# Other start addresses in SBUF for the softplus buffers, the staging buffers and the attention tiles

## The chip, the core and the metric

The kernel runs on one core of one Trainium2 chip. The metric is the device time of one execution in microseconds (us); a kernel's time is the median of several runs. The profile of one further execution shows where the time goes.

## The reference

Attention in chunks of 64 tokens (8 batches, 8 heads, 576 tokens, head size 64), and on its output, 4608 tokens by 512, a feed-forward layer with a softplus between two matrix products:

```python
scores = scale * np.matmul(q_c, k_c.transpose(0, 1, 2, 4, 3))   # chunks of 64 by 64
scores = scores - np.max(scores, axis=-1, keepdims=True)
attn = np.exp(scores)
attn = attn / (np.sum(attn, axis=-1, keepdims=True) + 1e-09)
out = np.matmul(attn, v_c)
...
h = x @ w_in                                                    # 4608x512 by 512x2048
g = np.maximum(h, 0.0) + np.log1p(np.exp(-np.abs(h)))           # softplus
return (g @ w_out).astype(np.float32)                           # 4608x2048 by 2048x512
```

## The kernel before

The tokens are cut into 9 macro tiles of 512, the 2048 columns of the hidden layer into 16 slices of 128. A block is one macro tile with one slice; there are 144. In each block TensorE makes two groups of matmuls. `gemm1` (line 567) makes a 128x512 piece of h: 12 matmuls, whose stationary operands (weights) are 128x128 pieces of w_in, in the tiles `wi_hi`, `wi_lo` or `wib`, and whose moving operands are pieces of `x`, the attention's output. `gemm2` (line 600) multiplies that block's softplus with w_out: 12 matmuls, whose weights are 128x128 pieces of `g_hi` and `g_lo`, and whose moving operands are rows of w_out (`wo_hi`, `wo_lo`, `late`, `wo_end`), 128x512. Each value stands as a sum of two float32r numbers, a high part and a low part, hence three matmuls for each product. (The first block is cut in two halves, `a0` and block 0.)

Between the two, ScalarE makes `u`, the softplus (line 578), and rounds it to `g_hi` (line 582), and VectorE or GpSimd takes the difference `g_lo` (line 586). `g_hi` and `g_lo` have two buffers each, `u` has one. TensorE's order is fixed: gemm1 of block n+1, then gemm2 of block n.

Attention works on tiles of 128 tokens by 512 (8 heads of 64). The first four are made at the start, in tiles that later hold weights (`late`, `x`). The others go through the loaded tiles `q` and `k`, the transposed ones `qe` and `ka` and the transposed probabilities `eT`. Their 64x64 matmuls stand between gemm1 and gemm2 of some blocks, as a burst (lines 449 and 530): the scores of two tiles and the output of the two before. A burst takes both buffers of the PSUM tile `pa`, which gemm1 takes as well. VectorE frees them with a maximum (line 494), a rest of x (line 546) and a subtraction (line 499).

Weights come in 32 loads into three staging buffers `raw` (lines 234 and 239), are put together in `top` and `low` (or `wib`) and rounded into their places (lines 247 to 286). The output is staged in `raw` too.

A planner with a table of costs makes the order of the instructions of all engines when the kernel is built; the addresses of tiles play no part in it. Pools of tiles lie one behind the other in each partition of SBUF, in the order in which they are opened, each tile rounded up to 32 bytes:

```python
later = ctx.enter_context(tc.tile_pool(name="later", bufs=2))
late = ctx.enter_context(tc.tile_pool(name="late", bufs=LATE))
const = ctx.enter_context(tc.tile_pool(name="const", bufs=1))
xpool = ctx.enter_context(tc.tile_pool(name="xpool", bufs=4))
ld = ctx.enter_context(tc.tile_pool(name="ld", bufs=1))
att = ctx.enter_context(tc.tile_pool(name="att", bufs=1))
sp = ctx.enter_context(tc.tile_pool(name="sp", bufs=2))
```

Of the kernel before, what the change touches and what calls it, by code (L numbers as in the profile page):

```python
# [11 lines left out]
F32 = mybir.dt.float32  # L12
F32R = mybir.dt.float32r
I32 = mybir.dt.int32
# [3 lines left out]
BF16 = mybir.dt.bfloat16  # L18
# [129 lines left out]
def chunked_attention_softplus_ffn(  # L148
# [12 lines left out]
    P = 128  # L161
# [14 lines left out]
    UW = 512  # L176
    RAW_BUFS = 3
# [2 lines left out]
    FILL = 0.8  # L180
    LATE = 15
    STAGED = 15

    later = ctx.enter_context(tc.tile_pool(name="later", bufs=2))
    late = ctx.enter_context(tc.tile_pool(name="late", bufs=LATE))
# [2 lines left out]
# [3 lines that stand above are left out]
# [5 lines left out]
    ident = const.tile([P, P], F32, name="ident")  # L196
    make_identity(nc, ident)
    half = DF // 2
    wi = [tuple(const.tile([P, KC, half], F32R, name=n) for n in ("wi_hi", "wi_lo"))]
    stage = [later.tile([P, KC * half], F32, name="wib") for _ in range(2)]  # L200
    wo_hi = const.tile([P, HALF_FC, DM], F32R, name="wo_hi")
# [19 lines left out]
    live = {}  # L221

    def raw_tile():
        return ld.tile([P, 2 * UW + 2], I32, name="raw", bufs=RAW_BUFS)

# [1 line left out]
    def w_load(u, is_in, fc):  # L229
        queue = nc.gpsimd if u in LOAD_POOL else nc.sync  # L230
        raw = raw_tile()
        st = raw.bitcast(U16)[:, 1 : 4 * UW + 1]
        if is_in:
            queue.dma_start(
                st.rearrange("p (c f) -> p c f", c=KC),
                w_in_v[:, :, 4 * fc * P : 4 * (fc + 1) * P],
            )
        else:
            queue.dma_start(st, w_out_v[:, fc, :])
        live["raw", u] = raw  # L240

    def w_top(u):
        live["top", u] = tops[0]
        tops.append(tops.pop(0))
        top = live["top", u].bitcast(F16).rearrange("p (f t) -> p f t", t=2)[:, :, 1]
        src = live["raw", u].bitcast(BF16)[:, 4:].rearrange("p (f t) -> p f t", t=4)[:, :, 0]
        (nc.gpsimd.tensor_copy if u not in TOP_ACT else nc.scalar.copy)(top, src)  # L247

    def w_low(u):
        if u < STAGED:  # L250
            o = u * UW
            low = stage[o // (KC * half)][:, o % (KC * half) :][:, :UW].bitcast(I32)
        else:
            low = ld.tile([P, UW], I32, name="low", bufs=LOW_BUFS)
        src = live.pop(("raw", u)).bitcast(U32)[:, 1 : 2 * UW + 1].rearrange("p (f t) -> p f t", t=2)[:, :, 0]
        nc.scalar.activation(low, src, AF.Copy, scale=2.0**-13)
        live["low", u] = low
# [347 lines left out]
    def evacuate(w, t):  # L605
        if t % 2 == 0:
            live["out", w["m"], t // 2] = raw_tile()
        o = live["out", w["m"], t // 2][:, t % 2 * DM : (t % 2 + 1) * DM].bitcast(F32)
        (nc.vector.tensor_copy if t % 2 else nc.scalar.copy)(o, pos[w["m"]][t])
        live["o", w["m"], t] = o  # L610
# [55 lines left out]
    for u, (g, is_in, fc) in enumerate(units):  # L666
        (of_in if is_in else of_out)[fc] = u
        d = due(g) - 4
        last = [f"w_hi{u}", f"w_lo{u}"]
        users = []  # L670
        if not is_in and fc >= HALF_FC:
            for j in range(2 * (fc - HALF_FC), min(2 * (fc - HALF_FC) + 2, LATE)):
                users.append("EVVSS"[j % 5] + str(j // 5))
        pl = "POOL" if u in LO_POOL else "DVE"
        ph_ = "POOL" if u in HI_POOL else "ACT"
        staged = u < STAGED
        pool = u in LOAD_POOL
        plan.add(f"load{u}", "POOL" if pool else "SP", 0.75 if pool else 0.55, partial(w_load, u, is_in, fc),
                 urg=d - LEAD if u else LQ, kb=480,
                 take=[("raw", [f"w_top{u}", f"w_low{u}"])], after=[LOAD_AFTER])  # L680
        on_act = u in TOP_ACT
        plan.add(f"w_top{u}", "ACT" if on_act else "POOL", 0.78 if on_act else 0.77, partial(w_top, u), [f"load{u}"],
                 urg=d, take=[("top", [f"w_add{u}"])])
        plan.add(f"w_low{u}", "ACT", 0.67, partial(w_low, u), [f"load{u}"], urg=d + 0.01,
                 take=[] if staged else [("low", last)], after=[f"w_top{u}"])
        plan.add(f"w_add{u}", "DVE", 0.68, partial(w_add, u), [f"w_top{u}", f"w_low{u}"], urg=d + 1.4, port=True)
        freed = []
        if is_in and fc == HALF_FC:
            freed = [f"w_{n}{j}" for n in ("hi", "lo") for j in range(STAGED)]
        if fc:  # L690
            freed.append(f"w_hi{(of_in if is_in else of_out)[fc - 1]}")
        plan.add(last[0], ph_, 0.63 if ph_ == "POOL" else 0.61, partial(w_hi, u, is_in, fc),
                 [f"w_add{u}"] + users + freed, urg=d + 2.1)
        plan.add(last[1], pl, 1.3 if pl == "POOL" else 0.65, partial(w_lo, u, is_in, fc, pl == "POOL"),
                 [last[0]] + users, urg=d + 2.8)
# [111 lines left out]
    for w in ahead + blocks:  # L807
        g, m, fc, name = w["g"], w["m"], w["fc"], w["name"]
# [58 lines left out]
```

## Time and profile before

| | |
|---|---|
| Time, median of 3 runs | 878.07 us (876.37 to 879.29) |
| The profiled execution's own time | 878.49 us |
| Its span, from the first to the last instruction | 876.7 us |
| TensorE (PE) matmuls | busy 861.6 us, 98% of the span |
| VectorE (DVE), ScalarE (ACT), GpSimd (POOL) | busy 348.5, 309.4 and 65.3 us |
| DMA engines | 31.9% of the span |

PE's share of busy time says little by itself: matmuls overlap, and each is shown from its start to a modelled end. How fast TensorE goes is read from the distance between the starts of matmuls that follow each other.

### The profile page before, as it was taken

How to read it: one execution, taken by the hardware profiler on the slowest of the kernel's cores; microseconds unless marked ns; L12 is line 12 of the kernel's file. 1: busy time of each engine (PE TensorE's matmuls, PEld its weight loads, DVE VectorE, ACT ScalarE, POOL GpSimd, SP SyncE). 2: the span in 40 equal slices, each digit the busy share in tenths (PEclk: the TensorE clock that was granted, in tenths of full speed). 3: DMA queues.
4: the chain of work that ended last, by engine and by line, in shares of the span. 5: the costliest groups of instructions: out<-in, count | busy, mean ns of one | idle time of the engine just before them, and what ended most of it. 6: DMA issues, size and time to landing. Idle time of an engine off the chain costs nothing.

```text
span 876.7 us, 14820 instructions
## 1 busy us (share of the span) xinstructions
PE 861.6 (98%) x5874; PEld 701.5 (80%) x5874; DVE 348.5 (40%) x589; ACT 309.4 (35%) x483; POOL 65.3 (7%) x68
## 2 busy tenths in 40 slices
PE   8799999999999999999999999999999999999998
PEld 7677888888888888888888888888888888888886
DVE  5999964333424161525242342334241614121111
ACT  4576744332423242424242332324232424222222
POOL 0564741000000000000000000000000000000000
PEclk9999999999999999999999999999999999999999
DMA  9787753322232224231322223122322241000001
GB/s 223 186 210 218 174 146 90 67 40 49 42 96 43 49 42 104 35 63 29 71 70 56 43 47 97 39 50 42 96 42 51 41 105 33 17 29 20 1 1 48
DMA packets 209958, 63.65 MB, mean 73 GB/s; under 512 B 187105, under 2 KB 203233, under 8 KB 209889
## 3 DMA queue, kind: packets, MB, share of 16 engines
q1 hardware_dynamic: 209888, 62.71, 31.9%
q8 instruction: 46, 0.75, 0.4%
q14 instruction: 24, 0.19, 0.1%
HBM read 45.09 MB, written 9.44 MB: 62 GB/s over the span
## 4 chain that ended last, share of the span: by engine, by line
PE 89%; DMA 4%; DVE 4%; SPq 1%; issue 1%; ACT 1%; POOL 0%; DVEq 0%; POOLq 0%; ACTq 0%
PE po L600 42%; PE pa L567 41%; PE pa L530 2%; DMA raw<-in_moe_w_in_dram 2%; PE pa L449 2%; DMA raw<-in_moe_w_out_dram 1%; PE po L330 1%; DVE wib L261 1%; SPq L322 1%; DVE mx L494 0%; DVE den L510 0%; DMA q<-in_q_dram 0%; DMA x<-in_v_dram 0%; DVE g_lo L586 0%; DVE x L546 0%
## 5 line engine op out<-in xcount | busy, mean ns | idle before, releaser
L578 ACT ACTIVATE u<-pa 128x512 f32<-128x512 f32 (+1 forms) x145 | 86.2, 594 | 510.1 <-PE pa L567 505.4
L586 DVE TENSOR_TENSOR g_lo<-u,g_hi 128x512 fp32r<-128x512 f32 (+1 forms) x137 | 94.9, 693 | 295.3 <-ACT g_hi L582 295.0
L567 PE MATMUL pa<-x,wib 128*128 128x512 f32 x864 | 208.6, 390 | 0.0
L567 PEld LDWEIGHTS pa<-x,wib 128*128 128x128 f32 x864 | 161.7, 188 | 36.0 <-PE po L600 2.4
L567 PE MATMUL pa<-x,wi_hi 128*128 128x512 f32 (+1 forms) x584 | 179.3, 389 | 2.1 <-DVE x L546 2.1
L600 PE MATMUL po<-late,g_hi 128*128 128x512 f32 x540 | 172.1, 394 | 0.0
L567 PEld LDWEIGHTS pa<-x,wi_hi 128*128 128x128 f32 x584 | 109.9, 189 | 24.3 <-DVE x L546 2.3
L600 PEld LDWEIGHTS po<-late,g_hi 128*128 128x128 f32 x540 | 101.2, 187 | 24.4
L567 PE MATMUL pa<-x,wi_lo 128*128 128x512 f32 (+1 forms) x292 | 114.0, 390 | 1.3 <-POOL top L247 1.0
L600 PE MATMUL po<-wo_hi,g_lo 128*128 128x512 f32 x288 | 114.9, 399 | 0.0
L600 PE MATMUL po<-late,g_lo 128*128 128x512 f32 x288 | 114.6, 398 | 0.0
L600 PE MATMUL po<-wo_lo,g_hi 128*128 128x512 f32 x288 | 114.0, 396 | 0.0
L600 PE MATMUL po<-wo_hi,g_hi 128*128 128x512 f32 x288 | 113.5, 394 | 0.0
L582 ACT CAST g_hi<-u 128x512 fp32r<-128x512 f32 (+1 forms) x145 | 89.4, 616 | 4.4
L567 PEld LDWEIGHTS pa<-x,wi_lo 128*128 128x128 f32 x292 | 55.2, 189 | 15.7 <-PE po L600 2.9
L600 PEld LDWEIGHTS po<-wo_hi,g_lo 128*128 128x128 f32 x288 | 54.3, 188 | 13.1
L600 PEld LDWEIGHTS po<-wo_hi,g_hi 128*128 128x128 f32 x288 | 54.1, 188 | 13.2
L600 PEld LDWEIGHTS po<-late,g_lo 128*128 128x128 f32 x288 | 54.0, 187 | 13.0
L600 PEld LDWEIGHTS po<-wo_lo,g_hi 128*128 128x128 f32 x288 | 54.1, 188 | 12.8
L494 DVE TENSOR_REDUCE mx<-pa 128x8 f32<-128x512 f32 x32 | 22.0, 686 | 69.4 <-ACT x L542 69.0
L426 DVE STREAM_TRANSPOSE qe<-q 128x512 f32<-128x512 f32 x29 | 20.5, 707 | 65.5 <-DMA k<-in_k_dram 46.3
L426 DVE STREAM_TRANSPOSE ka<-k 128x512 f32<-128x512 f32 x29 | 20.6, 711 | 51.1 <-DMA k<-in_k_dram 33.8
(101 smaller groups left out, 565.9 us busy)
## 6 DMA issues: line engine op xcount, KB each, us to landing
out_dram<-raw SPq DMA_DIRECT2D x36, 256.0 KB, 2.4
raw<-in_moe_w_in_dram SPq DMA_DIRECT2D x16, 512.0 KB, 5.0
raw<-in_moe_w_out_dram SPq DMA_DIRECT2D x16, 512.0 KB, 5.0
eT<-ka SPq DMA_DIRECT2D x248, 32.0 KB, 1.9
q<-in_q_dram SPq DMA_DIRECT2D x232, 32.0 KB, 2.2
k<-in_k_dram SPq DMA_DIRECT2D x232, 32.0 KB, 2.1
q<-in_v_dram SPq DMA_DIRECT2D x60, 64.0 KB, 2.5
k<-in_v_dram SPq DMA_DIRECT2D x60, 64.0 KB, 2.5
```

Of the source, the lines that this page charges most:

```text
L261: nc.vector.tensor_tensor(low, low, live.pop(("top", u)), op=ALU.add)
L322: nc.sync.dma_start(dv[a * C : (a + 1) * C, :, c2, :], v[b, a * HP : (a + 1) * HP, c * C : (c + 1) * C, :].rearrange("h s d -> s h d"),)
L330: nc.tensor.matmul(dst[:, :P], ident, ident, start=True, stop=True)
L426: nc.vector.transpose(t, live.pop((n, i)))
L449: nc.tensor.matmul(pa[o, c2, col : col + C], qT[r, a * HP + hl, :], kT[r, a * HP + hl, :], start=True, stop=True,)
L494: nc.vector.tensor_reduce(mx, sc, axis=AX.X, op=ALU.max)
L530: nc.tensor.matmul(pa[o, a, col : col + C], vt[r, 4 * j + 2 * h2 + c2, :], eT[r, :, 4 * c2 + 2 * j + h2, :], start=True, stop=True,)
L567: nc.tensor.matmul(ph, wt[:, c, fs], x[:, ts_, c, :], start=(n == 0), stop=(n == 3 * KC - 1))
L578: nc.scalar.activation(w["u"], w["ph"], AF.Softplus)
L582: nc.scalar.copy(w["hi"], w["u"])
L586: (nc.gpsimd if pool else nc.vector).tensor_tensor(w["lo"], w["u"], w["hi"].bitcast(F32), op=ALU.subtract)
L600: nc.tensor.matmul(pos[w["m"]][t], gg[:, ts_], wt, start=(w["first"] and n == 0), stop=(w["last"] and n == 2),)
```

## The change

Three edits of address alone. Each `raw` buffer gets 14 columns (56 bytes) more, which nobody reads or writes; with that the bounds of one slice in `w_top` are written out. Ahead of the softplus buffers stands a tile of 192 bytes, `pad`, which nobody uses. No instruction is added, dropped or moved: the instructions of every engine, with their waits, stand in the same order as before.

```diff
     STAGED = 15
+    G_PAD = 48
...
     half = DF // 2
+    sp.tile([P, G_PAD], F32, name="pad", bufs=1)
...
     def raw_tile():
-        return ld.tile([P, 2 * UW + 2], I32, name="raw", bufs=RAW_BUFS)
+        return ld.tile([P, 2 * UW + 16], I32, name="raw", bufs=RAW_BUFS)
...
-        src = live["raw", u].bitcast(BF16)[:, 4:].rearrange("p (f t) -> p f t", t=4)[:, :, 0]
+        src = live["raw", u].bitcast(BF16)[:, 4 : 4 * UW + 4].rearrange("p (f t) -> p f t", t=4)[:, :, 0]
```

What it does to the addresses follows from the sizes. The first pool begins at byte 16512 of each partition, which is 32 times 512 and 128 over. All tiles up to the staging buffers are multiples of 512 bytes, so they all stand at remainder 128 by 512.

| Tiles | Remainder by 512 before | after | Remainder by 64 before | after |
|---|---|---|---|---|
| `wib`, `late`, `wi_hi`, `wi_lo`, `wo_hi`, `wo_lo`, `wo_end`, `top`, `x` | 128 | 128 | 0 | 0 |
| `raw`, three buffers (4104 bytes, then 4160) | 128, 160, 192 | 128, 192, 256 | 0, 32, 0 | 0, 0, 0 |
| `q`, `k`, `low`, `eT`, `qe`, `ka` (2048 bytes) | 224 | 320 | 32 | 0 |
| `u`, `g_hi`, `g_lo` (2048 bytes) | 352 | 128 | 32 | 0 |

## Rows read from the trace of the kernel before

**Rows 1.** The page's chain of work that ended last: shares of the span by engine.

```profile
PE 89%; DMA 4%; DVE 4%; SPq 1%; issue 1%; ACT 1%; POOL 0%; DVEq 0%; POOLq 0%; ACTq 0%
```

**Rows 2.** Timeline of PE from 137.5 us: start, length, line, tiles; both in us.

```profile
137.50 0.39 PE L600 MATMUL po<-wo_hi,g_lo 128*128 128x512 f32 x1
...
138.20 0.40 PE L600 MATMUL po<-wo_hi,g_lo 128*128 128x512 f32 x1
...
138.90 0.39 PE L600 MATMUL po<-wo_hi,g_lo 128*128 128x512 f32 x1
...
139.60 0.40 PE L600 MATMUL po<-wo_hi,g_lo 128*128 128x512 f32 x1
...
140.29 0.39 PE L567 MATMUL pa<-x,wi_lo 128*128 128x512 f32 x1
...
140.97 0.39 PE L567 MATMUL pa<-x,wi_lo 128*128 128x512 f32 x1
...
141.65 0.39 PE L567 MATMUL pa<-x,wi_lo 128*128 128x512 f32 x1
...
142.33 0.39 PE L567 MATMUL pa<-x,wi_lo 128*128 128x512 f32 x1
...
143.02 0.39 PE L600 MATMUL po<-wo_hi,g_lo 128*128 128x512 f32 x1
```

**Rows 3.** The chain that ended last, in order of time: start, length (us).

```profile
213.95 3.00 PE po L600 x12
216.94 2.98 PE pa L567 x12
219.93 2.79 PE po L600 x12
222.72 2.73 PE pa L567 x12
...
730.14 2.98 PE pa L567 x12
```

**Rows 4.** Windows, instructions of line 600 alone: stretch, its length, busy (count).

```profile
84.00:877.00 793.00, 406.28 (x1644) 306.92 (x1644) 1.00 0.27 59
```

**Rows 5.** Timeline of all engines around 80 us; in brackets idle time and its releaser.

```profile
81.62 1.28 PE L530 MATMUL pa<-eT,x 64*64 64x64 f32 x29 [0.59 <-DMA x<-in_v_dram]
...
84.20 0.51 PE L530 MATMUL pa<-eT,x 64*64 64x64 f32 x19 [0.59 <-DMA x<-in_v_dram]
```

**Rows 6.** Timeline of all engines from 400 us: a subtraction, and gemm1 behind it.

```profile
402.75 0.68 DVE L499 TENSOR_TENSOR qe<-pa,mx 128x512 f32<-128x512 f32 x1
...
403.57 2.99 PE L567 MATMUL pa<-x,wib 128*128 128x512 f32 x12
```

**Rows 7.** Timeline of all engines from 406 us: the softplus of a block.

```profile
406.65 0.60 ACT L578 ACTIVATE u<-pa 128x512 f32<-128x512 f32 x1 [5.43 <-PE pa L567]
...
407.94 0.69 DVE L586 TENSOR_TENSOR g_lo<-u,g_hi 128x512 fp32r<-128x512 f32 x1 [3.19 <-ACT g_hi L582]
...
411.93 0.39 PE L600 MATMUL po<-late,g_lo 128*128 128x512 f32 x1
```

**Rows 8.** Timeline of POOL at 107 us: low weights of slice 13.

```profile
107.32 1.30 POOL L286 TENSOR_TENSOR wib<-low,wib 128x512 fp32r<-128x512 f32 x1
```

**Rows 9.** Timeline of PE at 110 us: gemm1 of slice 13.

```profile
110.14 1.07 PE L567 MATMUL pa<-x,wib 128*128 128x512 f32 x4
```

**Rows 10.** Groups of instructions of VectorE: busy us, mean ns, then idle time.

```profile
L546 DVE TENSOR_TENSOR x<-pa,x 128x512 fp32r<-128x512 f32 x36 | 23.2, 680 | 0.0
...
L609 DVE COPY raw<-po 128x512 f32<-128x512 f32 x18 | 11.7, 680 | 3.1 <-PE po L600 3.1
```

**Rows 11.** Timeline of PE from 13 to 22 us: the 64x64 matmuls of the scores.

```profile
15.29 1.09 PE L364 MATMUL po<-late 64*64 64x64 f32 x30
...
20.61 1.09 PE L364 MATMUL po<-ka,qe 64*64 64x64 f32 x30
```

**Rows 12.** DMA issues up to 130 us: count, KB each, median us to landing.

```profile
q<-in_q_dram SPq DMA_DIRECT2D x32, 32.0 KB, 3.9
...
x<-in_q_dram SPq DMA_DIRECT2D x8, 32.0 KB, 3.8
```

## The prediction

> **What bounds the kernel now.** I read the chain of work that ended last first. The reader is to see that TensorE alone makes 89% of it [rows 1]: apart from the start, the time is the distance between matmuls, added up. So the next view is the timeline of TensorE in a quiet stretch, and there not the lengths, which are modelled, but the starts [rows 2]. They stand three matmuls apart. In gemm1 three steps take 0.68 us, 0.2267 us each: 140.29, 140.97, 141.65, 142.33. In gemm2 three steps take 0.70 us, 0.2333 us each: 137.50, 138.20, 138.90, 139.60. Both groups stream 512 columns with a weight load for each matmul, so they should go at one pace, and gemm2 doesn't.
>
> The last three steps of each group tell on what that hangs. Those of gemm2, up to the first matmul of gemm1, take 0.69 us (139.60 to 140.29), less than its others. Those of gemm1, up to the first matmul of gemm2, take 0.69 us too (142.33 to 143.02), more than its others. In the last step of a group the moving operand is still its own, and the weights being loaded meanwhile are those of the next group. So the longer step goes with weights that come from `g_hi` and `g_lo`, and not with the moving operand or with the PSUM bank written. One block (137.50 to 143.02) takes 5.52 us; at gemm1's pace throughout, 8 times 0.68, it would take 5.44. That is 0.08 us in each of the 144 blocks.
>
> What sets weights in g apart from those in `wi_hi`, `wi_lo` and `wib` is their address: remainder 352 by 512 bytes, which is 32 by 64, against 128, which is 0 by 64. Both are 128x128 float32r with 512 bytes in a row in each partition. They also lie at the upper end of SBUF and were written shortly before, which the change leaves as it is.
>
> **The change, part by part.** No instruction, wait or DMA is added or moved, so every term is a duration that may change with an address.
>
> *The softplus buffers, 352 to 128.* The step with weights from g at remainder 128 isn't in the trace. From below I bound it by gemm1's 0.2267 us, whose weights stand at 128, from above by today's 0.2333 (nothing gained). I take 0.2267, since the last steps of gemm2 come nearest to the new state, `wo` moving and weights at 128 being loaded, and they go at the faster pace within what 0.01 us resolves: 0.69 for two slow steps and a fast one. Gain: 0.08 us a block, where TensorE is what the block waits for.
>
> *Where it isn't.* At 81.62 and 84.20 us TensorE waits 0.59 us each for v from HBM [rows 5]; whatever the blocks ahead save, it would wait longer there. Behind 84 us stand 1644 of gemm2's 1728 matmuls [rows 4], or 137 blocks. Behind twelve bursts gemm1 takes 2.92 to 2.98 us instead of 2.73, the first at 216.94 and the last at 730.14 [rows 3]: it needs a `pa` buffer, and begins at 403.57, right behind the subtraction that reads that buffer until 402.75 + 0.68 = 403.43 [rows 6]. That subtraction stands in a VectorE chain which the end of the burst starts, so gemm2 in between may go faster and gemm1 begins no earlier. Those twelve blocks gain nothing. There remain 125 blocks by 0.08, 10.0 us.
>
> *Does something else become late?* The softplus of a block begins at 406.65, `g_lo` is there at 408.63, and its gemm2 begins at 411.93 [rows 7]: 3.3 us to spare, and a block shortens by 0.08. While weights come in, the tightest place I found is slice 13: its low part is ready at 108.62 [rows 8], and gemm1 needs it at 110.14 [rows 9], 1.5 us later. Seven blocks between 84 and 126 us bring TensorE 0.6 us forward, so the cover holds; if it were gone at once, these seven would gain nothing, 0.6 us of the sum.
>
> *Staging, q, k, probabilities.* VectorE writes 128x512 from PSUM in 680 ns into `x` (remainder 128) and in 680 ns into `raw` (128, 160 and 192 mixed) [rows 10]. Thirty 64x64 matmuls of the scores take 1.09 us out of `late` at 128 and 1.09 us out of `ka` and `qe` at 224 [rows 11]. Loads of q in small pieces land after 3.8 us in `x` and 3.9 us in `q` at 224 [rows 12], in stretches of different load. I take nothing for all of these. As bounds, 0.1 us on such a load is hidden where q and k are loaded many blocks ahead; ahead of 84 us, where TensorE does wait for DMA, ten such loads in a row would be 1 us either way.
>
> *Sum.* The profiled execution takes 878.49 us, 876.7 of span and 1.8 around it. Less 10.0 that is 868.5. It stands 0.4 us above the median of 878.07, so I predict a median of 868.1 us.
>
> **Rows against the skill.** The trace has weights loaded from g going with a step longer by 0.0067 us. The Trainium skill, "TensorE: Matmul & The Clock Gate", section "Step-by-step: what each phase is for", says that TensorE reads weights and moving operand through two independent ports, so that loading the next weights takes no bandwidth from the running matmul. By that rule an address of g would cost nothing and the sum would be 0; the trace's last steps of a group speak against it. The same skill, "SBUF — State Buffer", section "Specifications (TRN2)", gives lines of 16 bytes. Both 352 and 128 are multiples of 16, so by that too nothing would change; no row here separates 16 bytes from 64.
>
> **The rivals.**
>
> 1. *No change, about 878.1 us.* The slower step belongs to g for another reason than its remainder: its place at SBUF's end, or that it is written and read within one block. For it: the scores' 64x64 matmuls go equally fast at remainders 128 and 224 [rows 11], which differ by 32 bytes beyond a multiple of 64 just as 128 and 352 do. Against it: each of these uses a quarter of the array, four in turn, so a longer load may be hidden behind the other three, and they load half the columns only. The two rules of the skill above would end here. Chance 0.10.
>
> 2. *Half, about 873 us.* Two things add up in g's 0.0067 us, and the remainder is one of them: 125 blocks by 0.04 are 5.0 us. Nothing in the rows shows two parts. Chance 0.08.
>
> 3. *Slower, about 888 us.* Now both streams of gemm2 stand at the same remainder by 512. If weights and moving operand then collide, a step becomes longer than today's 0.2333 us. If it grew by as much again as it now lies above gemm1's, 125 blocks by 0.08 would come on top. It decides from any step over 0.2333 on. Against it: gemm1 has weights at 128 and `x` at 128 or 384 (pieces of 256 bytes) and takes the faster step throughout, and in the last step of gemm2 both are at 128. Chance 0.05.
>
> 4. *The gain is made and eaten by waits* that I hold for covered: only the seven blocks above, 868.7 us; it belongs to the forecast.
>
> **How the numbers follow.** The forecast has the rest, 0.77, and by the spread of runs (876.4 to 879.3, 1.7 below and 1.2 above the median) its own range is 866.4 to 869.7. If the early and the twelve blocks gain as well, 144 by 0.08 are 11.5 us, which with that spread ends at 865.0. Upwards I go to 874.0, which takes in the half case and 1 us of it for loads at the start. That leaves out no change and slower, 0.15, and a little below. A change of 0.3% (2.6 us) is what a measurement of this kernel can tell from none. Faster by more than that: 0.77 + 0.08 = 0.85. Within: 0.10. Slower: 0.05.
>
> **What would show it.** In the profile after, three steps of gemm2 take 0.68 us like those of gemm1, also across the border between the two; a pair of gemm1 and gemm2 in the chain takes 5.44 us, not 5.52. The twelve gemm1 behind bursts begin as late behind their burst as now, so these are longer, by up to 0.08 us. The groups of ScalarE and VectorE keep their means within 10 ns, and the waits for v stay, together longer by some 0.6 us, the saving of the seven blocks ahead of them. If gemm2's three steps still take 0.70 us, the remainder isn't the cause and the prediction fails; if they shrink and the time doesn't, a wait has taken the gain, and the list of gemm1's late starts must show where.

## The result and the profile after

The changed kernel takes 868.39 us (median of 4 runs, 866.78 to 870.07) beside 877.35 us before (4 runs): ratio 0.9895, 95% interval 0.9866 to 0.9925. The forecast was 868.1 us and faster. The profiled execution took 869.51 us, 867.7 of span, against 878.49 and 876.7.

The page's chain, shares by engine, answers to [rows 1]; TensorE is still what everything else is hidden behind:

```profile
PE 88%; DMA 5%; DVE 4%; ACT 1%; issue 1%; SPq 1%; POOL 0%; DVEq 0%; POOLq 0%; ACTq 0%
```

The timeline of PE in the same stretch as [rows 2] (start and length in us; gemm1 is now line 569, gemm2 line 602):

```profile
137.40 0.39 PE L602 MATMUL po<-wo_hi,g_lo 128*128 128x512 f32 x1
...
139.44 0.39 PE L602 MATMUL po<-wo_hi,g_lo 128*128 128x512 f32 x1
...
140.12 0.39 PE L569 MATMUL pa<-x,wi_lo 128*128 128x512 f32 x1
...
142.84 0.39 PE L602 MATMUL po<-wo_hi,g_lo 128*128 128x512 f32 x1
```

Nine steps of gemm2 take 2.04 us (137.40 to 139.44), where they took 2.10 (137.50 to 139.60 in [rows 2]). The three steps across the border to gemm1 take 0.68 (139.44 to 140.12). The twelve of gemm1, its border included, take 2.72 (140.12 to 142.84) instead of 2.73 (140.29 to 143.02). The chain in order of time answers to [rows 3]:

```profile
213.11 2.94 PE po L602 x12
216.10 2.99 PE pa L569 x12
219.09 2.72 PE po L602 x12
221.81 2.72 PE pa L569 x12
...
400.50 2.99 PE pa L569 x12
```

A block is 2.72 + 2.72 = 5.44 us instead of 5.52. The gemm1 behind a burst is as late as before. VectorE's two rests of x and its subtraction ahead of that gemm1 are these rows of its timeline:

```profile
398.47 1.28 DVE L548 TENSOR_TENSOR x<-pa,x 128x512 fp32r<-128x512 f32 x2
399.67 0.68 DVE L501 TENSOR_TENSOR qe<-pa,mx 128x512 f32<-128x512 f32 x1
```

The subtraction ends at 400.35, and gemm1 begins 0.15 us behind it, at 400.50; in [rows 6] it was 0.14 us.

### The profile page after: what moved, and what is told of

It reads as the page before. It is cut to its first block, busy times and chain, and to the rows that moved or that the text cites. A ratio compares the mean times of both kernels' runs of the same rounds, so it can differ in the third digit from the quotient of the medians.

```text
span 867.7 us, 14820 instructions
## 1 busy us (share of the span) xinstructions
PE 850.9 (98%) x5874; PEld 701.5 (81%) x5874; DVE 347.6 (40%) x589; ACT 309.9 (36%) x483; POOL 64.7 (7%) x68
## 4 chain that ended last, share of the span: by engine, by line
PE 88%; DMA 5%; DVE 4%; ACT 1%; issue 1%; SPq 1%; POOL 0%; DVEq 0%; POOLq 0%; ACTq 0%
PE pa L569 42%; PE po L602 42%; DMA raw<-in_moe_w_out_dram 3%; PE pa L532 2%; PE pa L451 1%; DMA raw<-in_moe_w_in_dram 1%; DMA eT<-ka 1%; DVE wib L263 1%; PE po L332 1%; DVE g_lo L588 0%; SPq L324 0%; ACT u L580 0%; DVE mx L496 0%; DVE low L263 0%; DMA k<-in_v_dram 0%
## 5 line engine op out<-in xcount | busy, mean ns | idle before, releaser
L602 PE MATMUL po<-late,g_hi 128*128 128x512 f32 x540 | 169.5, 390 | 0.0
```

The source lines that it names most:

```text
L602: nc.tensor.matmul(pos[w["m"]][t], gg[:, ts_], wt, start=(w["first"] and n == 0), stop=(w["last"] and n == 2),)
```

## The experiments

All are the changed kernel with the edit shown; the last has none. The theories A, B, P and R are named in the expectations. The distance named below is that from the moving operand's start to the weights' start, by 128 bytes: 96 before the change (352 less 128), 0 after. Experiments of one group ran beside the same runs of the kernel before.

**1. The pad alone** (`e1_pad_only`)

```diff
-    G_PAD = 48
+    G_PAD = 72
...
-        return ld.tile([P, 2 * UW + 16], I32, name="raw", bufs=RAW_BUFS)
+        return ld.tile([P, 2 * UW + 2], I32, name="raw", bufs=RAW_BUFS)
```

> Only the softplus buffers move, to remainder 128 by 512; raw, q, k, low, qe, ka and eT stay where they were before. If the whole gain comes from weights read out of g (my theory), three steps of gemm2 take 0.68 us and the time is that of the changed kernel, 868 us, within 2 us. If the staging buffers or q, k and the probabilities have a part in it, it lies above that by their part: over 870 us.

Measured: 870.39 us, just over the 870 us that the expectation set as the limit, beside 878.36 before. The ratio is 0.9895 (0.9876 to 0.9913), that of the whole change. Its timeline of PE, nine steps of gemm2 in 2.04 us:

```profile
138.83 0.39 PE L602 MATMUL po<-wo_hi,g_lo 128*128 128x512 f32 x1
...
140.87 0.39 PE L602 MATMUL po<-wo_hi,g_lo 128*128 128x512 f32 x1
```

From gemm2 of block 14 to the end the span is 741.4 us here (869.2 less 127.80) and 741.3 in the first profile after (867.7 less 126.39), so from there on the whole gain is made. The gain is that of g's place; the wider staging buffers and the new places of q, k and the probabilities have no part in it that these runs could show.

**2. The staging buffers alone** (`e2_raw_only`)

```diff
-    sp.tile([P, G_PAD], F32, name="pad", bufs=1)
```

> The wider raw buffers without the pad: everything but g as in the changed kernel, and u and g at remainder 448 by 512, which is 0 by 64 but not that of w_out's tiles. Theory A (what counts is a start at a multiple of 64 bytes): three steps of gemm2 take 0.68 us, 868 us. Theory B (what counts is the same remainder by 512 as the other operand): 0.70 us, 877 to 878 us.

Measured: 881.3 us, ratio 1.0025 (1.0013 to 1.0038), slower than before the change, which neither theory had foreseen. Nine steps of gemm2 take 2.10 us, and nine of gemm1 (line 568) behind it 2.07, where they took 2.04 in [rows 2]:

```profile
136.12 0.40 PE L601 MATMUL po<-wo_hi,g_lo 128*128 128x512 f32 x1
...
138.22 0.39 PE L601 MATMUL po<-wo_hi,g_lo 128*128 128x512 f32 x1
...
138.92 0.39 PE L568 MATMUL pa<-x,wi_lo 128*128 128x512 f32 x1
...
140.99 0.39 PE L568 MATMUL pa<-x,wi_lo 128*128 128x512 f32 x1
```

Theory A, a start at a multiple of 64 bytes, is out. The distance is 64 here, and it costs more than the 96 before the change: gemm1 suffers as well.

**3. g at 96 by 512** (`e3_g_at_96`)

```diff
-    G_PAD = 48
+    G_PAD = 40
```

> The changed kernel with a pad of 160 bytes instead of 192: u and g at remainder 96 by 512, which is 32 by 64, and only 32 bytes from where they are after the change. Theory A: gemm2 is back at 0.70 us for three steps, 877 to 878 us. If the remainder was not the cause, or nearness to the remainder of w_out's tiles is enough, it stays at 868 us.

Measured: 878.46 us, ratio 0.9998 (0.9985 to 1.0011). All the other tiles are where the change puts them, and the gain is gone:

```profile
137.45 0.39 PE L602 MATMUL po<-wo_hi,g_lo 128*128 128x512 f32 x1
...
139.55 0.40 PE L602 MATMUL po<-wo_hi,g_lo 128*128 128x512 f32 x1
```

**4. g 16 bytes further** (`e4_g_plus_16`)

```diff
-        return sp.tile([P, MT], F32R, name=name, bufs=LAG + 1)[:, : w["cols"]]
+        return sp.tile([P, MT + 16], F32R, name=name, bufs=LAG + 1)[:, 4 : w["cols"] + 4]
```

> The changed kernel with g_hi and g_lo read and written 16 bytes behind a multiple of 64 (each buffer 64 bytes longer, so all four are alike). Theory A: off a multiple of 64 by 16 costs like 32, 0.70 us for three steps of gemm2 and 877 to 878 us. By the Trainium skill, SBUF page, section Specifications, lines are 16 bytes; by that a start at a multiple of 16 costs nothing, and it stays at 868 us. If the cost goes with the distance, it lies between, near 873 us.

Measured: 873.28 us, ratio 0.9931 (0.9915 to 0.9947), in the middle, but not for the reason given: the longer buffers lie apart by an odd multiple of 64, so the two buffers of each tile of g, which the blocks take in turn, differ. Two gemm2 that follow each other, timeline of PE:

```profile
137.66 0.39 PE L602 MATMUL po<-wo_hi,g_lo 128*128 128x512 f32 x1
...
139.75 0.39 PE L602 MATMUL po<-wo_hi,g_lo 128*128 128x512 f32 x1
...
143.16 0.39 PE L602 MATMUL po<-wo_hi,g_lo 128*128 128x512 f32 x1
...
145.20 0.39 PE L602 MATMUL po<-wo_hi,g_lo 128*128 128x512 f32 x1
```

The first takes 2.09 us for nine steps, the second 2.04. By the sizes, g_hi and g_lo begin at 208 and 336 by 512 in the blocks of even number and at 144 and 272 in those of odd number: their distances by 128 are 80 and 16. At 144 and 272 alike the step is fast, so the same remainder by 512 (theory B) isn't needed either; by 128 all runs so far agree: 0 and 16 fast, 64, 80 and 96 slow.

**5. The moving operand 64 bytes further** (`e5_wo_plus_64`)

```diff
+    const.tile([P, 16], F32, name="gap1")
     wo_hi = const.tile([P, HALF_FC, DM], F32R, name="wo_hi")
     wo_lo = const.tile([P, HALF_FC, DM], F32R, name="wo_lo")
+    const.tile([P, 112], F32, name="gap2")
```

> The changed kernel with wo_hi and wo_lo 64 bytes further (remainder 192 by 512), all other tiles where the change has them. They are gemm2's moving operands in slices 0 to 7; slices 8 to 15 use late and wo_end at 128. Theory P (the weights' own position by 128 bytes counts): nothing changes, three steps 0.68 us, 868 to 870 us. Theory R (the distance between weights and moving operand by 128 bytes counts): gemm2 of slices 0 to 7 goes at 0.70 us for three steps, 8 to 15 at 0.68; some 70 blocks by 0.08 us, 873 to 875 us.

Measured: 874.49 us, ratio 0.9947 (0.9929 to 0.9964). The chain in order of time, slices with `wo_hi` and then those with `late`:

```profile
175.28 2.76 PE po L604 x12
178.04 2.77 PE pa L571 x12
...
186.34 2.72 PE po L604 x12
189.06 2.72 PE pa L571 x12
```

The weights haven't moved, and gemm2 (line 604) is slower where its moving operand has. What neither theory had foreseen: gemm1 (line 571) of these slices is slower too, though its own tiles stand at distance 0. In these rows the two take 0.09 us more than 5.44. From gemm2 of block 14 on, with 64 such blocks, the span is 746.5 us (874.9 less 128.40) instead of 741.3, so 5.2 us or 0.08 a block.

**6. gemm1's weights 64 bytes further** (`e6_wi_plus_64`)

```diff
+    const.tile([P, 16], F32, name="gap1")
     wi = [tuple(const.tile([P, KC, half], F32R, name=n) for n in ("wi_hi", "wi_lo"))]
...
+    const.tile([P, 112], F32, name="gap2")
     wo_hi = const.tile([P, HALF_FC, DM], F32R, name="wo_hi")
```

> The changed kernel with wi_hi and wi_lo 64 bytes further (remainder 192 by 512), all other tiles where the change has them. They are gemm1's weights in slices 0 to 7; slices 8 to 15 use wib at 128. Theories P and R: gemm1 of slices 0 to 7 goes at 0.70 us for three steps, 8 to 15 at 0.68, 873 to 875 us. If the slow step belongs to g alone (its place in SBUF, or being written shortly before), nothing changes, 868 to 870 us.

Measured: 873.71 us, ratio 0.9952 (0.9936 to 0.9967). The chain, slices with `wi_hi` and then those with `wib`:

```profile
153.57 2.75 PE po L604 x12
156.31 2.80 PE pa L571 x12
...
183.64 2.72 PE po L604 x12
186.36 2.72 PE pa L571 x12
```

gemm1 takes 2.80 us where its weights stand 64 bytes off, 2.72 where they don't. So the slow step needs neither g's place at SBUF's end nor its being fresh. gemm2 of these slices, at distance 0, takes 2.75, again unforeseen.

**7. Everything 64 bytes further** (`e7_all_plus_64`)

```diff
+    later.tile([P, 16], F32, name="front", bufs=1)
     ident = const.tile([P, P], F32, name="ident")
```

> The changed kernel with every tile 64 bytes further, by a tile of 64 bytes ahead of the first pool's others: weights and moving operands all at remainder 192 by 512, which is 64 by 128. Theory P: both gemm1 and gemm2 take 0.70 us for three steps, some 0.16 us a block, 886 to 892 us. Theory R: the distances are as before, 0.68 us in both, 868 to 870 us.

Measured: 867.6 us, ratio 0.9883 (0.9868 to 0.9897). Twelve steps of gemm2 (line 603) take 2.72 us and nine of gemm1 (line 570) 2.04:

```profile
135.08 0.39 PE L603 MATMUL po<-wo_hi,g_lo 128*128 128x512 f32 x1
...
137.80 0.39 PE L570 MATMUL pa<-x,wi_lo 128*128 128x512 f32 x1
...
139.84 0.39 PE L570 MATMUL pa<-x,wi_lo 128*128 128x512 f32 x1
```

Theory P, the weights' own position, is out. With experiment 5 this leaves R: the distance between the two streams, the weights and the moving operand.

**8 and 9. Other distances** (`e8_g_32_48`, `e9_g_112_124`)

```diff
+    SHIFT = (8, 12)
...
     def g_tile(w, name):
-        return sp.tile([P, MT], F32R, name=name, bufs=LAG + 1)[:, : w["cols"]]
+        n = live["n", name] = 1 - live.get(("n", name), 1)
+        o = SHIFT[n]
+        return sp.tile([P, MT + 32], F32R, name=name, bufs=LAG + 1)[:, o : w["cols"] + o]
```

The second has `SHIFT = (28, 31)`.

> The changed kernel with g_hi and g_lo 32 bytes behind a multiple of 128 in one of their two buffers and 48 in the other (each buffer 128 bytes longer, so that all begin alike). The runs so far had the fast step at 0 and 16 behind, the slow one at 64, 80 and 96. If the border lies at 64, gemm2 of both parities takes 0.68 us for three steps and the time is near 868 to 870 us. If it lies at 32, both take 0.70 us, near 878 us; between them, one of each, near 873 us.

> The changed kernel with g_hi and g_lo 112 bytes behind a multiple of 128 in one of their two buffers and 124 in the other (each buffer 128 bytes longer). So far gemm2's step was fast at 0 and 16 behind, slow at 32, 48, 64, 80 and 96. If the fast range lies to both sides of 0, 124 and perhaps 112 are fast: 0.68 us for three steps in one or both parities, 868 to 874 us. If it begins at 0, both are slow, near 878 us.

Measured: 877.11 and 875.41 us (one run each, beside 878.2 and 878.33). Timeline of PE with 32 and 48, two gemm2 that follow each other:

```profile
137.43 0.39 PE L605 MATMUL po<-wo_hi,g_lo 128*128 128x512 f32 x1
...
139.49 0.39 PE L605 MATMUL po<-wo_hi,g_lo 128*128 128x512 f32 x1
...
142.93 0.39 PE L605 MATMUL po<-wo_hi,g_lo 128*128 128x512 f32 x1
...
145.02 0.40 PE L605 MATMUL po<-wo_hi,g_lo 128*128 128x512 f32 x1
```

and with 112 and 124:

```profile
137.33 0.39 PE L605 MATMUL po<-wo_hi,g_lo 128*128 128x512 f32 x1
...
139.37 0.39 PE L605 MATMUL po<-wo_hi,g_lo 128*128 128x512 f32 x1
...
142.78 0.39 PE L605 MATMUL po<-wo_hi,g_lo 128*128 128x512 f32 x1
...
144.88 0.39 PE L605 MATMUL po<-wo_hi,g_lo 128*128 128x512 f32 x1
```

The first of each pair is block 16, which in these programs has the second offset, the next is block 17 with the first. Nine steps take 2.06 us at 48 and 2.09 at 32, so neither is fast; 2.04 at 124, which is 4 bytes short of 0, and 2.10 at 112. The fast range reaches a little to both sides of 0. With 112 and 124 one gemm2 in two is fast, yet the time lies above the 868 to 874 us expected: the gemm1 behind the gemm2 at 112 is slower too, 2.76 us to the next gemm2 (145.57 to 148.33 in the same timeline).

**10. g_lo of the burst blocks on GpSimd** (`e10_glo_pool`)

```diff
-    GLO_POOL = (4,6,9,10,12,15,17,18)
+    GLO_POOL = (4,6,9,10,12,15,17,18) + tuple(range(22, 127, 8))
```

> The changed kernel with the g_lo of the blocks with a burst, from block 22 on, made by GpSimd instead of VectorE. My theory: behind bursts gemm1 waits for VectorE's subtraction, so no longer step of gemm2 ahead of it can be gained there; without g_lo in VectorE's chain the first subtraction ends over 0.6 us earlier, gemm1 comes without a wait, some 0.29 us in twelve blocks, and the time falls by 3 to 3.5 us against the changed kernel. Rival: gemm1 is late behind bursts for another reason (the other subtraction, or what TensorE does itself), and the time stays within 1 us of the changed kernel, or GpSimd's longer operation makes gemm2 wait and it rises.

Measured: 864.98 us, ratio 0.9846 (0.9829 to 0.9864), beside 868.41 for the changed kernel in the same group: 3.4 us less, and the fastest of all. Its timeline behind the burst at 395 us, and its chain behind the first of the twelve:

```profile
397.24 0.68 DVE L501 TENSOR_TENSOR qe<-pa,mx 128x512 f32<-128x512 f32 x1
...
397.83 0.68 DVE L548 TENSOR_TENSOR x<-pa,x 128x512 fp32r<-128x512 f32 x1
...
399.11 2.88 PE L569 MATMUL pa<-x,wib 128*128 128x512 f32 x12
```

```profile
216.05 2.72 PE pa L569 x12
```

The subtraction ends at 397.92, 1.2 us ahead of gemm1, and gemm1 takes 2.72 us instead of 2.99. That wait behind bursts was VectorE's. The edit does more than it says, though: with g_lo gone, the planner also put the subtraction ahead of the second rest of x (line 548), which it followed in the changed kernel. So it comes two operations of 0.6 us earlier, not one. With g_lo alone moved it would have ended some 0.6 us ahead of gemm1, by an estimate from these rows; that wasn't run.

**11. The changed kernel again** (`e11_changed_again`), without an edit.

> The changed kernel once more, beside the other two: 868 to 870 us, ratio 0.988 to 0.991 to the kernel before. Its trace should show again where the time of gemm2 ahead of 126 us went: TensorE waiting in the burst at 124 us, with gemm2 of block 14 beginning between 126 and 127 us, no earlier than in the kernel before.

Measured: 868.41 us, ratio 0.989 (0.9865 to 0.9916). Its timeline in the burst:

```profile
123.52 0.69 PE L532 MATMUL pa<-eT,k 64*64 64x64 f32 x32 [0.74 <-ACT u L580]
...
124.62 0.50 PE L602 MATMUL po<-late,g_lo 128*128 128x512 f32 x1
```

The wait is there again. But block 14 begins at 124.62, not between 126 and 127: the start of the program varies by more than the whole term of the early blocks, 0.6 us. What follows block 14 doesn't: 865.7 less 124.62 is 741.1 us here, 867.7 less 126.39 is 741.3 in the first profile after.

## Why the prediction was right, and where it was off

**The step of gemm2.** Right: 0.2267 us, as taken from the last steps of gemm2 in [rows 2]. The reading behind it, that the step goes with the weights and not with the moving operand, was half of it. It hangs on where the weights start against the moving operand, by 128 bytes: in experiment 5 the moving operand alone was moved, and the step grew; in experiment 7 both were, and it didn't. At 124 (4 short of the next 0), 0 and 16 the step is fast, at 32 to 112 slower. The last steps of gemm2 fit that too: weights and moving operand both stand at remainder 128 there. Some luck was in the choice of 128. What the prediction named beside it, a start at a multiple of 64, would have allowed 448 as well, where experiment 2 measured 881.3 us.

**The twelve blocks behind bursts.** Right: gemm1 takes 2.98 to 2.99 us there, where it took 2.92 to 2.98, and begins right behind VectorE's subtraction. Experiment 10 shows the cause by taking time out of VectorE's chain.

**The seven blocks between 84 and 126 us.** Here the step failed that checked the cover: "the cover holds", with 0.6 us for these blocks in the sum. Gemm2 of block 14 begins at 126.32 before and at 126.39 after. The rows of the kernel before:

```profile
122.51 0.69 ACT L256 ACTIVATE low<-raw 128x512 int32<-128x512 uint32 x1 [2.67 <-DMA raw<-in_moe_w_out_dram]
...
124.58 0.59 ACT L578 ACTIVATE u<-pa 128x512 f32<-128x512 f32 x1
...
125.23 0.69 PE L530 MATMUL pa<-eT,k 64*64 64x64 f32 x32
...
126.32 0.50 PE L600 MATMUL po<-late,g_lo 128*128 128x512 f32 x1
```

and of the changed one:

```profile
122.59 0.68 ACT L258 ACTIVATE low<-raw 128x512 int32<-128x512 uint32 x1 [3.81 <-DMA raw<-in_moe_w_out_dram]
...
124.65 0.59 ACT L580 ACTIVATE u<-pa 128x512 f32<-128x512 f32 x1
...
125.30 0.69 PE L532 MATMUL pa<-eT,k 64*64 64x64 f32 x32 [1.28 <-ACT u L580]
...
126.39 0.50 PE L602 MATMUL po<-late,g_lo 128*128 128x512 f32 x1
```

The burst's second half needs the `pa` buffer that the softplus `u` reads. On ScalarE `u` stands behind the staging of w_out's last slices (`low`), which waits for its load until 122.5 us before and 122.6 after. Before the change TensorE came just when `u` ended (124.58 + 0.59 = 125.17, and 125.23): there was no cover left. In the changed kernel it comes earlier and waits 1.28 us. Part of that isn't the change's doing, since gemm2 of block 7, ahead of these seven blocks, already begins 0.90 us earlier (84.27 instead of 85.17).

The other traces bear this out. In all thirteen that staging step waits for its load, and gemm2 of block 14 begins 3.79 to 3.82 us behind the step's start, though its time varies from 124.05 to 128.40 us. So what TensorE saves ahead of it is lost, unless the load comes sooner for it. That the traces can't tell: the staging step starts at 122.51 in both kernels with distance 96, and between 120.25 and 124.00 in the five with distance 0. The prediction asked when weights are ready and not what stands in ScalarE's queue ahead of the softplus; it is rival 4, in a place that it hadn't named. Another order of that queue wasn't tried.

**The sum.** From block 14 on the span falls from 750.4 us (876.7 less 126.32) to 741.3, by 9.1 us. Kernels with the same distances agree there: 750.3 in experiment 3, 741.1 to 741.4 in experiments 1, 7 and 11. These are 130 blocks; without the twelve 118, and 118 by 0.08 are 9.4. The two executions differ by 9.0, the medians by 9.0. The forecast's 10.0 was that and the seven blocks. That the time came within 0.3 us of the forecast is partly luck: the gain was 1.0 us smaller, and the kernel before was 0.7 us faster beside the change (877.35) than in the three runs that the forecast started from (878.07). The upper end of its own range should have been 869.3 (868.1 and 1.2), not 869.7. One of its signs didn't come: the waits for v, to be longer by some 0.6 us, were 1.2 us in all before and 0.9 after, and from 0.2 to 1.7 over the thirteen traces.

**The rivals.** No change: its argument from the 64x64 matmuls [rows 11] falls, since there both operands stand at 128 in the one row and both at 224 in the other, distance 0 in both. The Trainium skill ("TensorE: Matmul & The Clock Gate", section "Step-by-step: what each phase is for") has loads of weights and the running matmul on independent ports. This kernel's traces don't bear out that they leave each other alone: the step depends on where the two operands start against each other, by up to 0.007 us. Nor do the lines of 16 bytes of the Trainium skill ("SBUF — State Buffer", section "Specifications (TRN2)") explain it: distances 16 and 48 are both multiples of 16, and nine steps take 2.04 and 2.06 us. Slower: the same remainder for both streams is the fast place, the reverse of that rival. Half: not seen; the step fell by the whole 0.0067 us.

## What to carry to other kernels

Where each matmul comes with a weight load, compare the distance between starts of matmuls across the groups of one kernel, at equal column counts. A group that is slower by some per cent without a wait may stand badly in SBUF: try its weights and moving operand at the same remainder by 128 bytes. That was seen here with 128x128 float32r weights and 512 moving columns, and nothing else was tried. Before counting a faster engine's gain, go through the queues of the engines that it waits for in order of time, and count only the blocks behind the last wait that the faster engine doesn't shorten.

## What was unexpected

A slow group can slow the one behind it, although that one stands at distance 0: gemm1 takes 2.77 us instead of 2.72 in experiment 5, gemm2 2.75 in experiment 6. At a distance of 96 it doesn't: nine steps of gemm1 take 2.04 us in [rows 2].

Nor is 0.2267 us all that distance 0 gives. Behind a burst the changed kernel too needs some steps to come to its pace. In experiment 11 the second to sixth step of gemm2 of block 14 take 1.16 us, 0.232 each, where five by 0.2267 would be 1.13 (its timeline):

```profile
124.95 0.62 PE L602 MATMUL po<-late,g_hi 128*128 128x512 f32 x2
...
126.11 0.39 PE L602 MATMUL po<-late,g_lo 128*128 128x512 f32 x1
```

The distance doesn't give the whole cost either: at 64, a group takes 2.80 us in experiments 2 and 6 and 2.76 in experiment 5. Why the two streams disturb each other, and why the disturbance lasts, these runs don't show.
